# A fused attention, MoE and Fourier-mixing kernel: attention's steps, their router and the hand-over to the experts in another order

## The chip, the cores and the metric

The kernel runs on one core of one Trainium2 chip, in one launch. The metric is the device time of that launch in microseconds, as the median of the runs. The engines are TensorE (PE, with its weight loads PEld), VectorE (DVE), ScalarE (ACT), GpSimd (POOL) and SyncE (SP); SP issues most transfers, and a queue's waits are shown as SPq or POOLq.

## What is computed

Three layers follow each other: decayed attention without a softmax, a mixture of eight experts in which a token takes one expert, and a Fourier mixing with a channel MLP.

```python
# 1: q, k, v are (4, 8, 576, 64)
scores = scale * np.matmul(q, k.transpose(0, 1, 3, 2))
Dmat = np.where(rel >= 0, gamma[:, None, None] ** rel[None, :, :], 0.0)
x = np.matmul(scores * Dmat[None, :, :, :], v)          # as (4, 576, 512)
# 2: per token; e is its own argmax, or its predecessor's if the local gate is at least 0.5
logits = np.einsum('bsd,de->bse', x, w_gate)
local_gate = 1.0 / (1.0 + np.exp(-np.einsum('bsd,de->bse', x, w_local).squeeze(-1)))
out[b, s] = p[e] * (np.maximum(x[b, s] @ w1[e], 0.0) @ w2[e])
# 3
u = x + np.real(np.fft.fft(np.fft.fft(x, axis=1), axis=2))
out = u + np.maximum(norm(u) @ w_ch1, 0.0) @ w_ch2
```

## The kernel before

**Attention's steps.** Each of the four batches is cut into blocks of 128 tokens; STEPS lists 18 steps, four for block 0 of each batch (c = 0), then four for each later block, and at last two steps with two half blocks each. Blocks of one batch are tied by a state: `sp` = v'ks (L458), added on DVE to the running `sum` (L468, for c = 0 a copy, L466), which the next block's outputs read. The loop over the 18 steps writes all engines' work in the order in which they execute it. Step i does, on PE, the outputs o of step i-1 (L495 to L509: qg times the state, and am times v), then sp and the products a = kT'qT (L480) of step i, then `tr` (L524), which turns x of step i-1 by an identity with the gate's columns beside it. DVE turns a into am (L484, times the decay, in two halves), ACT copies o into xT (L516), which `tr` reads. `prep` (L429) makes qg and ks on POOL, two steps ahead.

**back.** From `tr` DVE sums the router's logits L (L527), ACT takes the largest magnitude (Abs, L536), DVE makes a scale mx from it (L537 to L546), ACT writes the scaled row's high half xh (L547) and DVE the low half xl (L549) into the row xr.

**route.** Once per four steps `route` runs as a generator beside the steps: m, ls, t, fr, cc on DVE (L558 to L567), ex on ACT, `row` on PE (L578, cc transposed), sm (L582 to L585), kr, er, e (L591 to L598) on DVE, et, oh, then the ranks rk on PE (L616 to L634), the gate (L641), and c8, sl, slot (L643 to L648), carry (L650). The slots are the places to which POOL's `scatter` (L666) sends the rows by indirect DMA; `fetch` (L685) reads the first expert's rows (called expert 8 below) back transposed.

**Beside the steps.** The weights of expert 8 come in eight pieces of 512 KB. `hook` (L2278) issues a piece per step from step 2 on, and at step 0 four DMAs that fill the rows' buffer with zeros. `beside` (L2296) converts the pieces: ACT takes `absmax` (L239) and writes a float16 high part (`high`, L281), DVE the rest (`low`, L286). 15 products on zeros (`warm`, L717) run on PE ahead of step 0.

**The end.** After step 17 PE runs hidden(f) (L815), expert 8's first products; relu's low half is a DVE instruction (L833) per f. DVE casts the tally of the router to n_i (L2108), from which SP takes the order of the other experts. Then `outputs` (L836) runs 24 products for each of two row tiles: for each f wh by the high and low hidden rows, and wl by the high ones. SP meanwhile loads the next expert's weights (`w1.load`, L229), the padding (L1006) and the rows xt and mt of the next two experts (`fetch`, L1047 and L1060). All of SP's queue goes in the order written.

## Time and profile before

| | before |
|---|---|
| median of three runs | 790.78 us (790.6, 790.78, 798.08) |
| the profiled execution | 787.88 us |
| its span | 785.7 us |
| PE busy | 724.8 us, 92% of the span |
| DVE busy | 592.3 us, 75% |
| ACT busy | 411.8 us, 52% |
| POOL busy | 126.8 us, 16% |

The page's chain that ended last is "issue" for 25% of the span. Attention takes the first 110 us, expert 8 the stretch to about 136, and the other experts follow from 139.86 us on. Times in rows are microseconds from the span's start; a row is one instruction or a run of equal ones, and brackets give the engine's idle time ahead of it and what ended it.

### The profile page before, as it was taken

What the parts mean: (1) busy time and instruction counts of PE and PEld (TensorE: products, weight loads), DVE (VectorE), ACT (ScalarE), POOL (GpSimd) and SP (SyncE); (2) the same over time, 40 slices, a digit from 0 to 9 for tenths busy, and PEclk for the clock granted to TensorE, in tenths of its full rate; (3) what the DMA queues carried; (4) which work ended last, traced back from release to release, by engine and by line L of the source; (5) the groups of instructions that cost most, each with busy time, mean ns of one, the idle gap of its engine ahead of it and who ended that gap; (6) DMA issues with size and microseconds to landing.
All of it is one profiled execution on the core that took longest, in us unless ns stands there. A gap on an engine that the chain in (4) does not pass through costs nothing. (4 is left out here: it accounts for less than half of the span.)

```text
span 785.7 us, 17150 instructions
## 1 busy us (share of the span) xinstructions
PE 724.8 (92%) x6529; PEld 542.8 (69%) x6529; DVE 592.3 (75%) x1432; ACT 411.8 (52%) x829; POOL 126.8 (16%) x225
## 2 busy tenths in 40 slices
PE   8888898899999998879998999899899999999996
PEld 5677685655566555557644448778788888888885
DVE  3678888589889988857898969958876695646462
ACT  1356657378888797845847526426332451414140
POOL 3566443002102201113000011010010001010101
PEclk9999999899999999999999999999999999999998
DMA  9998449999998998964427276600550017110000
GB/s 296 355 305 293 154 115 309 295 315 344 293 360 304 270 352 287 262 235 149 136 77 240 102 214 232 175 28 2 170 150 2 28 62 195 28 55 2 28 2 27
DMA packets 91929, 142.27 MB, mean 181 GB/s; under 512 B 48116, under 2 KB 49017, under 8 KB 90814
## 3 DMA queue, kind: packets, MB, share of 16 engines
q1 hardware_dynamic: 87246, 126.78, 51.4%
q0 software_dynamic: 4592, 14.31, 5.0%
q8 instruction: 53, 0.87, 0.4%
q14 instruction: 38, 0.31, 0.1%
HBM read 97.55 MB, written 35.12 MB: 169 GB/s over the span
## 5 line engine op out<-in xcount | busy, mean ns | idle before, releaser
L1666 PE MATMUL g<-gxt,wh 128*128 128x256 f16 (+1 forms) x992 | 143.6, 284 | 2.6 <-DMA gxt<-un 1.4
L2011 PEld LDWEIGHTS <-hd 128*128 128x128 f16 x1176 | 114.2, 98 | 26.9 <-issue 7.1
L1666 PEld LDWEIGHTS <-wh 128*128 128x128 f16 x1056 | 102.8, 98 | 28.5 <-issue 4.9
L286 DVE SCALAR_TENSOR_TENSOR wl<-wst,ws,wh 128x1024 f16<-128x1024 f32 (+1 forms) x82 | 100.3, 1253 | 8.1 <-ACT wh L281 8.0
L281 ACT ACTIVATE wh<-wst,ws 128x1024 f16<-128x1024 f32 x80 | 89.0, 1140 | 26.1 <-DVE ws L274 25.7
L815 PE MATMUL ps<-xt,wh 128*128 128x320 f16 (+4 forms) x544 | 79.1, 284 | 8.1 <-DMA xt<-xs 5.8
L845 PE MATMUL ps<-wh,hid 128*128 128x512 f16 (+2 forms) x528 | 84.6, 302 | 0.2 <-ACT hid L831 0.2
L2011 PE MATMUL g<-wh,hd 128*128 128x256 f16 x448 | 78.3, 273 | 4.3 <-DVE u L2040 2.0
L1666 PE MATMUL g<-gxt,wl 128*128 128x256 f16 (+1 forms) x496 | 80.5, 285 | 0.0
L815 PEld LDWEIGHTS <-wh 128*128 128x128 f16 x640 | 57.5, 100 | 33.2 <-issue 13.8
L1872 POOL DMA_INDIRECT out<-u,orow x18 | 17.9, 993 | 383.9 <-DVE u L2040 284.8
L845 PEld LDWEIGHTS <-hid 128*128 128x128 f16 (+2 forms) x792 | 46.4, 100 | 42.4 <-issue 2.7
L239 ACT ACTIVATE wh<-wst 128x1024 bf16<-128x1024 f32 x66 | 69.3, 1050 | 7.7 <-DVE wst L311 5.2
L2040 DVE SCALAR_TENSOR_TENSOR u<-g,ffs,u 128x256 f32<-128x256 f32 (+1 forms) x63 | 34.1, 568 | 49.3 <-PE g L2011 48.7
L1982 DVE SCALAR_TENSOR_TENSOR s<-g,r 128x256 f32<-128x256 f32 x168 | 53.3, 374 | 23.4 <-ACT hd L1976 22.7
L1955 ACT ACTIVATE hd<-s 128x640 f16<-128x640 f32 x56 | 41.3, 737 | 47.8 <-DVE s L1982 47.8
L1975 ACT ACTIVATE r<-g 128x256 f32<-128x256 f32 x56 | 21.1, 378 | 84.0 <-PE g L1666 78.0
L2011 PE MATMUL g<-e,hd 128*128 128x256 f16 x504 | 59.9, 273 | 5.0 <-DVE u L2040 4.0
L859 POOL DMA_INDIRECT x<-y,mt x25 | 31.5, 1261 | 194.7 <-ACT y L857 149.7
L2011 PE MATMUL g<-wl,hd 128*128 128x256 f16 x224 | 61.1, 273 | 0.0
L1666 PEld LDWEIGHTS <-wl 128*128 128x128 f16 x528 | 51.9, 98 | 11.7 <-issue 1.1
L845 PE MATMUL ps<-wl,hid 128*128 128x512 f16 (+2 forms) x264 | 56.4, 302 | 0.0
(299 smaller groups left out, 1280.7 us busy)
## 6 DMA issues: line engine op xcount, KB each, us to landing
wst<-in_moe_w SPq DMA_DIRECT2D x64, 512.0 KB
raw<-in_ch SPq DMA_DIRECT2D x14, 1024.0 KB
qk<-in_qkv SPq DMA_DIRECT2D x18, 512.0 KB
vk<-in_qkv SPq DMA_DIRECT2D x16, 512.0 KB
pair<-ch SPq DMA_DIRECT2D x32, 256.0 KB
ch<-d SPq DMA_DIRECT2D x14, 512.0 KB
wst<-ch SPq DMA_DIRECT2D x14, 512.0 KB
u<-u SPq DMA_DIRECT2D x9, 512.0 KB
```

The source lines that it names most:

```text
L239: self.nc.scalar.activation(out=x, in_=t, func=ACTF.Abs, accum_out=self.am[:, j : j + 1])
L281: self.nc.scalar.activation(out=self.dst[0][:, j, :], in_=self.pieces[j], func=ACTF.Copy, scale=self.by(j))
L286: self.nc.vector.scalar_tensor_tensor(out=l[:, j, c], in0=self.pieces[j][:, c], scalar=self.by(j), in1=h[:, j, c], op0=ALU.mult, op1=ALU.s ...
L815: nc.tensor.matmul(out=ps, lhsT=m[:, k, 128 * f : 128 * f + 128], rhs=xt[:, x + k, :], start=(k == 0 and i == 0), stop=(k == 3 and i == last),
L845: nc.tensor.matmul(out=ps[r * j : r * j + r, 0:d], lhsT=hid[x][:, f, 128 * t : 128 * t + r], rhs=m[:, 4 + f // 2, c : c + d], start=(f == ...
L859: nc.gpsimd.indirect_dma_start(out=x2[:, :].rearrange("t (k d) -> (t k) d", k=k), out_offset=bass.IndirectOffsetOnAxis(ap=mt, axis=0), in_ ...
L1666: nc.tensor.matmul(out=ps, lhsT=m[:, k + 4 * (f // 8), 128 * (f % 8) : 128 * (f % 8) + 128], rhs=xt[x][:, k, :], start=(k == 0 and i == 0) ...
L1955: nc.scalar.activation(out=hd[:, 0, 2:7], in_=s, func=ACTF.Copy, scale=C2 / 2)
L1975: nc.scalar.activation(out=r, in_=p[:, 1:3], func=ACTF.Relu)
L1982: V.scalar_tensor_tensor(out=d, in0=x, scalar=0.0, in1=y, op0=ALU.max, op1=op)
L2011: nc.tensor.matmul(out=ps, lhsT=hid[k][:, y, x, :], rhs=E[w][m][k], start=(k == 0 and m == y == 0), stop=(k == 7 and y == 1),)
L2040: V.scalar_tensor_tensor(out=y, in0=p, scalar=fs[:, c : c + 1], in1=y, op0=ALU.mult, op1=ALU.add)
```

## The change

In words: (1) Nine warm-up products instead of 15; the constants' loads change places (kd ahead of v, the identity's copies made by ACT, both gates in one array, the rest after step 1), and the zero-fill and the weights' pieces come at later steps. (2) In a step a stands ahead of sp, am ahead of the sum; the state's copies go to ACT and behind xh; the logits stand behind Abs; `high` gets in ahead of xh and `low` ahead of L. (3) A router's first part is taken up in the step after, behind `scores`; its parts from kr and from c8 on come behind xl. (4) Two `low` parts that ran as four halves in steps 16 and 17 run whole after the tally. (5) Expert 8's second products take wl's last. (6) SP fetches expert 0's rows ahead of the eighth piece of weights.

```diff
-WARM = 15
-FILLED = 4
+WARM = 9
+FILLED = 5
...
-HALVES = {16: [(4, 0)], 17: [(5, 0)]}, {16: [(4, 1)], 17: [(5, 1)]}
...
-    load(0)
-    kd = const("kd", [128, 4, 8], src=A["kd"].rearrange("p (c h) -> p c h", c=4))
+    kd = const("kd", [128, 4, 8])
+    load(0, lambda: nc.sync.dma_start(out=kd, in_=A["kd"].rearrange("p (c h) -> p c h", c=4)))
     dec = const("dec", [128, H, 128], src=A["dec"].rearrange("p (h q) -> p h q", h=H))
+    idw, idn = const("idw", [128, 4, 137]), keep.tile([128, 128], FP32, name="idn")
+    nc.sync.dma_start(out=idn, in_=A["idn"])
+    nc.sync.dma_start(out=idw[:, :, 128:137], in_=A["gates"].rearrange("p (c e) -> p c e", c=4))
+    nc.scalar.copy(out=idw[:, :, 0:128], in_=idn.unsqueeze(1).to_broadcast([128, 4, 128]))
     load(1)
...
-    idw = const("idw", [128, 4, 137])
-    nc.sync.dma_start(out=idw[:, :, 0:128], in_=A["idn"].unsqueeze(1).to_broadcast([128, 4, 128]))
-    nc.sync.dma_start(out=idw[:, :, 128:136], in_=A["w_gate"].rearrange("(c p) e -> p c e", p=128))
-    nc.sync.dma_start(out=idw[:, :, 136:137], in_=A["w_local"].rearrange("(c p) e -> p c e", p=128))
-    idn = keep.tile([128, 128], FP32, name="idn")
-    nc.sync.dma_start(out=idn, in_=A["idn"])
     load(2)
...
-            if c == 0:
-                V.tensor_copy(out=total[b][0], in_=sp)
-            else:
+            if c > 0:
                 V.tensor_tensor(out=total[b][c % 2], in0=sp, in1=total[b][(c - 1) % 2], op=ALU.add)
-            if c == 3:
-                for g in range(2):
+
+            def keep_state():
+
+                if c == 0:
+                    nc.scalar.copy(out=total[b][0], in_=sp)
+                for g in range(2) if c == 3 else ():
                     r = slice(64 * g, 64 * g + 64)
                     nc.scalar.copy(out=apart[b][r, :, r], in_=total[b][1][r])
...
         nc.scalar.activation(out=xh.bitcast(BF16), in_=tr, func=ACTF.Abs, accum_out=mx[:, 0:1])
+        if i < N - 1:
+            logits()
...
         V.reciprocal(out=mx[:, 2:3], in_=pi)
+        yield
         nc.scalar.activation(out=xh, in_=tr, func=ACTF.Copy, scale=mx[:, 2:3])
...
             rate()
+        if c < 3:
+            yield "amid"
         kr = W("kr", [C, 128], BF16)
...
         V.tensor_tensor(out=gate[:, at], in0=ps, in1=sm, op=ALU.mult)
+        if c < 3:
+            yield "amid"
         c8 = W("c8", [128, 2, 8])
...
-        scores(i)
+        kept = scores(i)
+        for g in fresh:
+            next(g)
+        live.extend(fresh)
+        fresh.clear()
...
+        next(r, None)
+        kept()
...
         if i % 4 == 0 and i > 0:
-            live.append(route(i // 4 - 1))
-            next(live[-1])
+            if i < 16:
+                fresh.append(route(i // 4 - 1))
+            else:
+                live.append(route(i // 4 - 1))
+                next(live[-1])
...
-    first.low(6)
-    first.low(7)
+    for j in range(4, 8):
+        first.low(j)
...
+    parts = ((h, 0), (h, 1), (l, 0))
+    each = [(f, i) for f in range(8) for i in range(3)]
+    if lows:
+        each.sort(key=lambda p: (p[1] == 2, p))
...
-    for p in range(6, 8):
-        w1.load(p)
+    w1.load(6)
     fetch(0)
+    w1.load(7)
     fetch(1)
...
-                if i == 0:
+                if i == 3:
...
-                if 2 <= i < 10:
-                    w.load(i - 2)
+                if 4 <= i < 12:
+                    w.load(i - 4)
```

How the order changes at three places. On DVE, around step 5 of attention, where the first router's part stands. Names: m to cc are the router's first part, sum the state, am the decayed scores, L the logits and mx the scale of the turned row. Before:

```order
L558 TENSOR_REDUCE m<-L 128x4
L560 TENSOR_TENSOR ls<-L,m 128x32
L563 SCALAR_TENSOR_TENSOR t<-ls,c_rt 128x32
L565 TENSOR_REDUCE fr<-t 128x4
L567 SCALAR_TENSOR_TENSOR cc<-L,fr 128x4
L569 CAST cc<-fr 1x4
L468 TENSOR_TENSOR sum_1_182<-sp,sum_0_181 128x256
L484 TENSOR_TENSOR am<-a,c_dec 128x4x128 x2
L527 TENSOR_REDUCE L<-tr 128x9
```

With the change, at the same place:

```order
L466 TENSOR_TENSOR am<-a,c_dec 128x4x128 x2
L481 TENSOR_TENSOR sum_1_178<-sp,sum_0_177 128x256
L576 TENSOR_REDUCE m<-L 128x4
L578 TENSOR_TENSOR ls<-L,m 128x32
L581 SCALAR_TENSOR_TENSOR t<-ls,c_rt 128x32
L583 TENSOR_REDUCE fr<-t 128x4
L585 SCALAR_TENSOR_TENSOR cc<-L,fr 128x4
L587 CAST cc<-fr 1x4
L539 TENSOR_REDUCE L<-tr 128x9
```

The router's six instructions stand behind the step's am and sum instead of ahead of them; on PE `row`, which reads cc, stands where it stood, behind `tr` and ahead of the next outputs.

On DVE behind the tally of the router, ahead of expert 8's second products (wl_78 the low hidden rows, one instruction an f; wl_76 the low part of a piece of the weights). Before:

```order
L2107 TENSOR_REDUCE wh_77<-wh_77 1x21
L2108 CAST n_i<-wh_77 1x20
L833 SCALAR_TENSOR_TENSOR wl_78<-r,wl_78 128x256
L286 SCALAR_TENSOR_TENSOR wl_76<-wst,ws,wh_75 128x1024 x2
L833 SCALAR_TENSOR_TENSOR wl_78<-r,wl_78 128x256 x3
```

With the change:

```order
L2149 TENSOR_REDUCE wh_77<-wh_77 1x21
L2150 CAST n_i<-wh_77 1x20
L871 SCALAR_TENSOR_TENSOR wl_78<-r,wl_78 128x256
L285 SCALAR_TENSOR_TENSOR wl_76<-wst,ws,wh_75 128x1024 x4
L871 SCALAR_TENSOR_TENSOR wl_78<-r,wl_78 128x256 x3
```

Four whole parts instead of two stand between the low hidden rows of f = 4 and those of f = 5 to 7.

On SP, from the reading of n_i on (wst a piece of the next weights, xs<-z the padding, xt and mt the rows of expert 0). Before:

```order
L2115 TENSOR_LOAD n_i
L2115 ISA x2
L1006 ISA
L1006 DMA xs<-z 32x9x528
L229 ISA
L229 DMA wst<-in_moe_w 128x2x512
L229 ISA
L229 DMA wst<-in_moe_w 128x2x512
L1047 DMA_TRANSPOSE xt<-xs 128x4x128 x2
L1060 DMA mt<-xs 128x2
```

With the change:

```order
L2157 TENSOR_LOAD n_i
L2157 ISA x2
L1048 ISA
L1048 DMA xs<-z 32x9x528
L228 ISA
L228 DMA wst<-in_moe_w 128x2x512
L1089 DMA_TRANSPOSE xt<-xs 128x4x128 x2
L1102 DMA mt<-xs 128x2
L228 ISA
L228 DMA wst<-in_moe_w 128x2x512
```

The transposes and mt stand ahead of the eighth piece instead of behind it; the six pieces ahead of n_i keep their place in SP's queue.

## Rows read from the trace of the kernel before

**Rows 1.** PE by line, 5.3 to 30.07: count, busy, mean ns, idle, releaser.

```profile
L458 PE MATMUL sp<-vk,ks 128*64 128x64 f32 x80 | 3.4, 228 | 3.1 <-POOL ks L441 3.0
L509 PE MATMUL o<-am,vk 128*64 128x128 f32 x64 | 5.7, 282 | 0.9 <-DVE am L484 0.9
L717 PE MATMUL warm<-z 128*128 128x512 f16 x8 | 2.2, 420 | 0.0
```

**Rows 2.** Windows: length, each engine's busy time (instructions), clock, DMA share, GB/s.

```profile
core 0: us, PE busy (x) PEld busy (x) DVE busy (x) ACT busy (x) POOL busy (x), PEclk, DMA share, GB/s
1.79:5.30 3.51, 3.51 (x9) 1.30 (x10) 0.00 (x0) 0.26 (x1) 1.94 (x5) 1.00 0.95 278
5.30:30.07 24.77, 20.54 (x264) 16.28 (x262) 12.06 (x30) 6.14 (x13) 7.25 (x7) 1.00 1.01 323
75.48:99.70 24.22, 19.81 (x306) 17.39 (x306) 21.22 (x67) 16.63 (x31) 13.20 (x24) 1.00 0.51 150
139.90:145.30 5.40, 5.40 (x52) 5.40 (x52) 0.82 (x3) 0.95 (x4) 0.00 (x0) 0.50 0.88 168
346.65:350.06 3.41, 3.41 (x9) 1.18 (x10) 3.24 (x11) 3.17 (x6) 0.00 (x0) 0.50 0.82 259
505.40:511.10 5.70, 2.82 (x25) 2.34 (x24) 5.56 (x16) 0.91 (x2) 0.00 (x0) 1.00 0.36 106
```

**Rows 3.** PE by line in 30.07:52.53, 52.53:75.48 and 75.48:99.7, one after another.

```profile
L524 PE MATMUL tr<-c_idw,xT 128*128 128x137 f32 x33 | 5.0, 291 | 2.8 <-ACT xT L516 1.6 <-DVE xr L549 1.2
...
L524 PE MATMUL tr<-c_idw,xT 128*128 128x137 f32 x33 | 5.0, 291 | 3.3 <-DVE xr L549 2.2 <-ACT xT L516 1.0
...
L524 PE MATMUL tr<-c_idw,xT 128*128 128x137 f32 x33 | 5.1, 291 | 4.4 <-ACT xT L516 2.9 <-DVE xr L549 1.5
...
L578 PE MATMUL row<-c_cb,cc 128*4 128x128 bf16 x1 | 0.2, 217 | 0.0
```

**Rows 4.** Timeline of PE: start, length, instruction, count, idle time before it.

```profile
110.06 0.61 PE L815 MATMUL ps<-wh,wh 128*128 128x256 f16 x4
...
124.94 0.60 PE L845 MATMUL ps<-wh,wl 128*128 128x512 f16 x2
...
139.86 0.37 PE L815 MATMUL ps<-xt,wh 128*128 128x128 f16 x2 [4.05 <-DMA xt<-xs]
...
346.65 0.59 PE L845 MATMUL bank<-wh,hidl 128*128 128x512 f16 x1 [3.95 <-PEq L2169]
```

**Rows 5.** Timeline of ACT in step 14.

```profile
90.44 0.69 ACT L547 ACTIVATE xr<-tr,mx 128x512 f16<-128x512 f32 x1 [1.47 <-DVE oh L605]
91.03 1.14 ACT L281 ACTIVATE wh<-wst,ws 128x1024 f16<-128x1024 f32 x1
```

**Rows 6.** Timeline of DVE in steps 13, 14 and 16.

```profile
83.42 0.59 DVE L583 TENSOR_SCALAR sm<-sm 128x4 f32<-128x4 f32 x1
...
86.42 0.41 DVE L468 TENSOR_TENSOR sum<-sp,sum 128x256 f32<-128x256 f32 x1
86.75 1.28 DVE L484 TENSOR_TENSOR am<-a,c_dec 128x512 f32<-128x512 f32 x2
...
103.29 0.18 DVE L558 TENSOR_REDUCE m<-L 128x4 f32<-128x32 f32 x1
...
104.25 0.16 DVE L567 SCALAR_TENSOR_TENSOR cc<-L,fr 128x4 bf16<-128x4 f32 x1
```

**Rows 7.** Timelines of DVE and of SP's queue: the rows of experts 8 and 0.

```profile
97.48 0.17 DVE L648 CAST c_slot_i<-c_slot_f 128x4 int32<-128x4 f32 x1
...
106.37 2.69 SPq L685 DMA_TRANSPOSE wh<-xs  x2
...
131.29 3.15 SPq L1047 DMA_TRANSPOSE xt<-xs  x2
```

**Rows 8.** Timeline of DVE: a half part of low in step 16, then the end.

```profile
100.54 0.75 DVE L286 SCALAR_TENSOR_TENSOR wl<-wst,ws,wh 128x512 f16<-128x512 f32 x1
...
125.30 2.46 DVE L286 SCALAR_TENSOR_TENSOR wl<-wst,ws,wh 128x1024 f16<-128x1024 f32 x2
127.69 0.41 DVE L833 SCALAR_TENSOR_TENSOR wl<-r,wl 128x256 f16<-128x256 f32 x1
```

More of the change, by code (lines that the diff above doesn't have):

```diff
@@ L443, in prep @@
             )
+        if c > 0:
+            qg = wk.tile([128, 4, 128], FP32, tag="qg", name="qg", bufs=3)
+            for j in range(len(lanes)):
+                w = slice(n * j, n * j + n)
+                nc.gpsimd.tensor_tensor(out=qg[:, :, w], in0=qT[:, :, w], in1=qds[c][:, :, 0:n], op=ALU.mult)
         pre[i] = (qg, ks)
@@ L719, in attention, with turn @@
     prep(1)
-    live = []
-    def turn():
-        for g in list(live):
-            if next(g, "end") == "end":
+    live, fresh, amid = [], [], []
+    def turn(of=None):
+        for g in list(live if of is None else of):
+            said = next(g, "end")
+            if said == "end":
                 live.remove(g)
-    level(1)
+            if said == "amid":
+                amid.append(g)
     for i in range(N):
@@ L747, in attention @@
             load(i + 3)
-        if i % 4 == 1 and 2 <= i // 4 + 2 <= 4:
-            level(i // 4 + 2)
+        if i % 4 == 0 and i < 16:
+            level(i // 4 + 1)
+        if i == 1:
+            rest()
         turn()
         next(r, None)
+        turn(amid)
+        amid.clear()
         if i > FILLED:
@@ L1129, in moe @@
     for t in range(2):
-        out(weights(0), hid0, mt0, fs, t, n, (parts,) if t else (), partial(w1.spread, 0) if t else None, 0)
+        out(weights(0), hid0, mt0, fs, t, n, (parts,) if t else (), partial(w1.spread, 0) if t else None, 0, True)
     v = weights(2)
@@ L2312, in beside @@
                     w.low(i - 12)
-                for j in HALVES[0].get(i, ()):
-                    w.low(*j)
                 yield
@@ L2319, in beside @@
                     w.high(j)
-                for j in HALVES[1].get(i, ()):
-                    w.low(*j)
                 yield
```

88 lines of the change are left out of this document (48 added, 40 removed).

## The prediction

> **What bounds the kernel now.** I read the table of busy time first: TensorE (PE) is by far the busiest engine, and the chain that ended last is mostly issue time on PE, so what can be won is PE's waiting. I then listed PE's idle time line by line for the stretch that the change rewrites, attention and the hand-over to the experts (0 to 145 us), and looked in the timelines of VectorE (DVE), ScalarE (ACT) and SyncE (SP) at who ended each wait. Behind 145 us no edit touches anything and PE is nearly dense, so I carry a shift at expert 0 unchanged to the end.
>
> [...] In steps 0 to 4 PE waits 3.1 us at sp, nearly all for ks on GpSimd (POOL), whose v block comes late, and 0.9 us at o for am [rows 1], while the DMA engines are full (share 1.01) and DVE is busy only 12.06 of 24.77 us [rows 2]. In steps 5 to 16 `tr` waits 2.8, 3.3 and 4.4 us in three cycles of four steps, half of it for the copy xT on ACT and half for xl on DVE, and `row` waits nothing [rows 3]. [...]
>
> **Term 1, the start (steps 0 to 4).** Fewer loads and broadcasts of constants stand between qk1 and qk2, kd comes ahead of v, the zero-fill's four DMAs go from step 0 to step 3, the pieces of the first weights start two steps later, POOL makes ks ahead of qg, and a stands ahead of sp on PE. All of it aims at the 4.0 us of waits for ks and am. The bytes ahead of step 4 fall little and the engines are full, so it can't all vanish; and the state's first copy, which leaves DVE, now stands on ACT behind xh and ahead of xT, on the chain tr, Abs, L, mx, xh, xT. I take half, 2.0 us, with 0.5 and 3.0 as bounds. What the moves delay: a piece now has two steps instead of four until `absmax` reads it on ACT. At about 5 us a step that is some 10 us, and I cost it at nothing; if a piece is late, ACT waits for the difference, and behind it xT and `tr`.
>
> **Term 2, cycles of four steps.** The conversion `high` (1.14 us) now runs between Abs and xh, in the 1.47 us that ACT idles ahead of xh [rows 5], instead of between xh and xT: that takes about 1.1 us off xT in steps 11 to 14. The sum stands behind am, and kr, er, e and the slots behind xl, so `tr` waits less for DVE. Against it, the first part of the router, m to cc, moves from the end of step 4k to behind am and the sum of step 4k+1, while its reader `row` keeps its place on PE, between `tr` and the next outputs. From a's end DVE needs 1.3 us for am, 0.33 for the sum and 1.1 for m to cc, 2.7 in all [rows 6]. PE meanwhile has sp (3.4 us in five steps, 0.7) and tr (5.0 in four, 1.2) [rows 1, 3], and reaches `row` after 1.9. So `row` waits 0.8 us where it waited nothing; where small operations stretch as one did to 0.59 [rows 6], more, and I put the upper bound at 2.0. I take 1.5 a cycle, nearer to it, since POOL works on ks and qg in just these steps. In each of the first two cycles I leave some 0.4 of waits for xT, so they win 2.8 - 1.5 - 0.4 = 0.9 and 3.3 - 1.5 - 0.4 = 1.4. In the third DVE is busy 21.22 of 24.22 us [rows 2], and no DVE work leaves it: at most 3.0 can be won, and with the router's part in its busiest step I take 0.5. Sum 2.8 us, bounds 0 (the new waits eat all) and 5.5 (`row` at 0.8, little left over).
>
> **Term 3, the rows for hidden(0).** The first expert's rows hang on the slots of step 15: cast at 97.48, transposes issued at 106.37 [rows 7], first product at 110.06 [rows 4], 12.6 us that nothing shortens. The cast now stands behind xl (0.67 us), so it gains 0.7 less than the steps do: 2.0 + 2.8 - 0.7 is 4.1, and I say 4.0 us at hidden(0).
>
> **Term 4, expert 8's second products.** Four half parts of `low` go from steps 16 and 17 (0.75 us each) to behind the tally's cast, as two whole parts ahead of the low hidden rows f5 to f7. Two parts took 2.46 us, so f5's rows, which started at 127.69, start 2.46 later and are there at about 130.5 [rows 8]. The block has 48 products from 124.94 to 135.81 (the wait ahead of 139.86 taken off), 0.226 each [rows 4]; with the wl products last PE wants f5's low rows after eleven, at 127.4. It waits 3.1 us and ends the block near 138.7 instead of 135.8. The DVE time freed earlier lies where hidden(0) waits for rows, so I count nothing for it. [...]
>
> **Term 5, rows for expert 0.** The two transposes leave their place behind the eighth piece. SP issued them at 131.29 [rows 7], and xt was read at 139.86 [rows 4], 8.6 us later. Now pieces 4 and 5 wait for `low` 4 and 5, the seventh for `low` 6 (125.30 + 3 x 1.23 = 129.0 [rows 8]), then come the transposes: issue about 129.5, landed by 138.1 at the same latency, sooner without 512 KB ahead of them. PE comes at 138.7, so the 4.05 us wait is gone, and the low clock behind it. But 3.1 us of idle time now lie inside expert 8's products. After 3.95 us idle [rows 4] the clock stood at 0.50 for 3.41 us; a stretch with 2.9 us idle in two pieces kept 1.00 [rows 2]. I count one such stretch, 1.7 us, with 0 and 2.7 as bounds.
>
> **The sum**, at expert 0: before, 139.86 and 2.7 lost behind it, 142.6. After, 138.7 - 4.0 + 1.7 = 136.4. Gain 6.2 us. The profiled execution took 787.88 us, its span 785.7; the sum takes it to about 781.7. The median of the runs, 790.78, lies 2.9 above that execution; less 6.2 it is **784.6 us**. With all terms at their low ends the gain is 0.5 + 0 - 0.7 + 3.9 - 2.7 = 1.0, at their high ends 3.0 + 5.5 - 0.7 + 3.9 = 11.7.
>
> **Rivals.**
> *Attention gives all, and the clock holds.* Term 1 at 2.3, term 2 at 4.5, no half-rate stretch: 2.3 + 4.5 - 0.7 + 3.9 = 10.0, 780.8. For it: the xT waits can go by order alone. Against: DVE is busy 88% in the third cycle.
> *The waits only change their name.* `row` waits 2.0 us a cycle, DVE is the bound in all of them, and term 1's 0.7 is taken back by the slots: nothing at hidden(0). The wait in expert 8 brings the longer clock loss: 3.9 - 2.7 = 1.2, 789.6. For it: the 10.5 us were split evenly over two engines, and relief of one leaves the other.
> *Slower: the clock at the start.* Nine warm-up products instead of 15. Until 5.30 us nine of them took 3.51 us [rows 2], 0.39 each where expert 8's take 0.226, so they ran near the lower level (though the clock column says 1.00 there). If the clock does not hold behind so short a lead, steps 0 to 4 run at half speed for a while: their PE work is 20.54 us [rows 2] less the warm-up's 2.2 [rows 1], 18.3 or 3.7 a step, and each such step costs 3.7 more, less the idle time in it. Term 1 is gone then; the other 4.2 us of gain are gone once the extra work passes the 4.0 us of idle time by 4.2, from 2.2 steps on. With all five steps it is 18.3 - 4.0 - 4.2 = 10.1 over before, 801. Against: the clock had risen by 5.30, with eight or nine of the 15 done, and from there to 30.07 it stood at 1.00 with 4.2 us idle. [...]
> *The fetch stays last.* If the transposes land at 140.0 as before, less 4.0, PE at 136.4 waits for nothing either, or 1.3 us if the clock held: inside the forecast's spread.
>
> **How the numbers follow.** Forecast 0.47 (own range 781.5 to 788), all of attention 0.25 (777.5 to 782.5), renamed waits 0.21 (788 to 792), slow start 0.05, anything else 0.02. A change of 1% (7.9 us, about what a measurement of this kernel can tell from none) lies at 782.9 and 798.7. Below fall nearly all of the second case and a sixth of the first, 0.32; above only part of the slow start, 0.04. Range 778 to 791.
>
> **What would show it.** Step 4's outputs start on PE near 28 us; `row` waits 1 to 2 us three times, and `tr` no more than 1 us in each of cycles one and two; hidden(0) starts near 106; a wait of about 3 us for DVE's hidden rows lies between two products of expert 8, and none for xt ahead of expert 0. If `tr` still waits for xl, term 2 is wrong; if expert 0 waits for xt over 1 us, term 5; if the block of expert 8 is dense, term 4; if PE is busy for well over 20 us of the time to step 5, the slow start is there.

## The result, and the profile after

| | before | changed |
|---|---|---|
| median of 20 runs each | 791.92 us (788.0 to 798.08) | 795.82 us (790.96 to 801.7) |
| the profiled execution | 787.88 us | 800.71 us |
| its span | 785.7 us | 798.9 us |
| its mean granted clock | 0.988 | 0.979 |
| PE busy / DVE / ACT / POOL | 724.8 / 592.3 / 411.8 / 126.8 us | 733.1 / 591.6 / 413.7 / 129.5 us |
| step 4's outputs start | 30.1 us | 29.94 us |
| step 16's outputs start | 99.8 us | 102.81 us |
| hidden(0) starts | 110.06 us | 114.38 us |
| expert 8's second products, expert 0, expert 1 start | 124.94, 139.86, 152.95 us | 130.21, 146.06, 156.86 us |

The change takes 1.0052 times as long as before, with the interval from 1.0031 to 1.0074: about 4 us lost where 6.2 were to be won, and 4.8 us above the range. The profiled execution lies 4.9 us above the median of the changed kernel; its distance at expert 1, 3.9 us, is that of the medians, and what it loses behind expert 1 is its own in large part (see What stays open).

PE by line in the three cycles of four steps, one after another (columns as in [rows 3]), and sp in the start:

```profile
L473 PE MATMUL sp<-vk,ks 128*64 128x64 f32 x80 | 3.4, 227 | 3.2 <-POOL ks L439 2.3 <-issue 0.4 <-POOL qg L446 0.4
...
L532 PE MATMUL tr<-c_idw,xT 128*128 128x137 f32 x33 | 5.1, 292 | 0.0
...
L596 PE MATMUL row<-c_cb,cc 128*4 128x128 bf16 x1 | 0.2, 218 | 1.9 <-DVE cc L587 1.9
...
L532 PE MATMUL tr<-c_idw,xT 128*128 128x137 f32 x33 | 5.0, 290 | 1.5 <-DVE kr L611 1.5
...
L596 PE MATMUL row<-c_cb,cc 128*4 128x128 bf16 x1 | 0.2, 218 | 1.0 <-DVE cc L585 1.0
...
L532 PE MATMUL tr<-c_idw,xT 128*128 128x137 f32 x33 | 5.0, 288 | 5.1 <-ACT xT L524 3.4 <-DVE kr L611 1.8
...
L596 PE MATMUL row<-c_cb,cc 128*4 128x128 bf16 x1 | 0.2, 217 | 0.8 <-DVE cc L585 0.8
```

`row` waits 1.9, 1.0 and 0.8 us where it waited nothing. `tr` waits nothing in the first cycle and 1.5 in the second, where [rows 3] had 2.8 and 3.3, but 5.1 in the third, where it had 4.4. The 3.1 us of [rows 1] at sp have become 3.2.

Windows of the changed kernel (columns as in [rows 2]): a stretch inside the start, one inside the third cycle, and one inside expert 8.

```profile
11.20:14.60 3.40, 3.40 (x30) 3.00 (x28) 0.00 (x0) 0.59 (x1) 0.61 (x1) 0.50 0.99 389
...
96.60:100.00 3.40, 3.40 (x33) 3.07 (x32) 2.97 (x13) 2.73 (x6) 0.18 (x1) 0.50 0.02 5
...
137.50:140.90 3.40, 3.40 (x10) 1.19 (x9) 0.98 (x7) 0.00 (x0) 0.00 (x0) 0.50 1.06 297
```

The start has a stretch at a granted clock of 0.50 that [rows 2] don't have, the third cycle another, 1.5 us behind the end of a wait of 2.56 us (at 95.08, shown below). Timeline of PE at the hand-over, answering [rows 4]:

```profile
114.38 1.04 PE L853 MATMUL ps<-wh,wh 128*128 128x256 f16 x4 [1.62 <-DMA wh<-xs]
...
135.80 1.77 PE L887 MATMUL ps<-wh,wl 128*128 128x512 f16 x5 [3.06 <-DVE wl L871]
...
146.06 1.11 PE L853 MATMUL ps<-xt,wh 128*128 128x128 f16 x17
```

The wait inside expert 8 is there with 3.06 us, half rate behind it (the window at 137.50), and expert 0 starts without the 4.05 us.

All of PE's time can be sorted into idle time (gaps in its timeline), what half rate cost (an estimate: half of the busy time at a granted clock of 0.50; the first 52 products of expert 0 take 5.46 us at it before, 3.14 in g3 of the experiments) and work (the rest), in us, from 1.79 on. Up to 5.30 us before and 7.81 in the changed kernel the clock column says 1.00, but products take longer than later (16 of a at 5.75 take 2.20 us in the changed kernel, 1.16 later), so I count PE's busy time there as half rate, 1.76 and 3.01 us of the first row:

| stretch | before: idle / half rate / work | changed: idle / half rate / work | difference |
|---|---|---|---|
| to step 4's outputs | 4.23 / 1.76 / 22.28 | 3.53 / 4.72 / 19.90 | -0.1 |
| to step 16's outputs | 10.54 / 0 / 59.15 | 10.57 / 1.71 / 60.59 | +3.2 |
| to hidden(0) | 0.36 / 0 / 9.94 | 1.62 / 0 / 9.94 | +1.3 |
| to expert 1 | 6.09 / 2.70 / 34.11 | 5.09 / 3.04 / 34.35 | -0.4 |
| to the end | 37.9 / 3.4 / 591.4 | 43.2 / 7.1 / 591.8 | +9.2 |

In the twelve steps from step 4 to 16 the idle time is what it was, 10.5 us under other names. Two columns of this table had no term in the prediction's attention: half rate (+4.7 up to step 16) and work (+1.4 in the twelve steps). The table sets one execution beside one, and its first row does not hold for others (see Point by point); in the twelve steps the difference does: they take 68.1 to 70.0 us in three traces that have before's steps up to there (before, and e3 and g3 of the experiments) and 72.9 to 73.5 in three that have the changed ones (changed, e4, g4).

### The profile page after: what moved, and what is told of

Its sections match the earlier page's. It is cut to its first block, busy times and chain, and to the rows that moved or that the text cites. A ratio compares the mean times of both kernels' runs of the same rounds, so it can differ in the third digit from the quotient of the medians.

```text
span 798.9 us, 17114 instructions
## 1 busy us (share of the span) xinstructions
PE 733.1 (92%) x6523; PEld 545.8 (68%) x6523; DVE 591.6 (74%) x1426; ACT 413.7 (52%) x834; POOL 129.5 (16%) x225
## 5 line engine op out<-in xcount | busy, mean ns | idle before, releaser
L285 DVE SCALAR_TENSOR_TENSOR wl<-wst,ws,wh 128x1024 f16<-128x1024 f32 x80 | 100.1, 1283 | 7.5 <-ACT wh L280 6.2
L280 ACT ACTIVATE wh<-wst,ws 128x1024 f16<-128x1024 f32 x80 | 89.1, 1141 | 31.7 <-DVE ws L273 31.6
L1914 POOL DMA_INDIRECT out<-u,orow x18 | 17.9, 996 | 384.0 <-DVE u L2082 286.2
L2082 DVE SCALAR_TENSOR_TENSOR u<-g,ffs,u 128x256 f32<-128x256 f32 (+1 forms) x63 | 34.1, 567 | 49.3 <-PE g L2053 47.5
L2053 PE MATMUL g<-e,hd 128*128 128x256 f16 x504 | 61.6, 277 | 5.0 <-DVE u L2082 4.0
```

The source lines that it names most:

```text
L280: self.nc.scalar.activation(out=self.dst[0][:, j, :], in_=self.pieces[j], func=ACTF.Copy, scale=self.by(j))
L285: self.nc.vector.scalar_tensor_tensor(out=l[:, j, c], in0=self.pieces[j][:, c], scalar=self.by(j), in1=h[:, j, c], op0=ALU.mult, op1=ALU.s ...
L1914: nc.gpsimd.indirect_dma_start(out=out[:, :], out_offset=bass.IndirectOffsetOnAxis(ap=orow[:, r // 128 : r // 128 + 1], axis=0), in_=o, in ...
L2053: nc.tensor.matmul(out=ps, lhsT=hid[k][:, y, x, :], rhs=E[w][m][k], start=(k == 0 and m == y == 0), stop=(k == 7 and y == 1),)
L2082: V.scalar_tensor_tensor(out=y, in0=p, scalar=fs[:, c : c + 1], in1=y, op0=ALU.mult, op1=ALU.add)
```

## The experiments

The second column is the ratio to the kernel before, run on the same chip. The third is the mean time of a run at half rate, worked out from each run's mean granted clock and span, (1 - clock) x 2 x span, an estimate that takes the clock to be either 1.00 or 0.50, the levels of the windows above; before has 22.6 to 23.7 us, the changed kernel 29.7. It counts the time at that level whether PE works or stands idle.

| label | ratio, 95% interval | us at half rate |
|---|---|---|
| e1_start | 1.0005 [0.9970, 1.0040] | 27.4 |
| e2_steps | 1.0081 [1.0046, 1.0115] | 33.3 |
| e3_end | 0.9999 [0.9976, 1.0023] | 19.5 |
| e4_warm15 | 1.0047 [1.0027, 1.0067] | 24.7 |
| f1_sm_late | 1.0036 [1.0007, 1.0066] | 31.7 |
| f2_route_old | 1.0021 [0.9997, 1.0045] | 32.3 |
| f3_qg_first | 1.0089 [1.0063, 1.0114] | 32.1 |
| f4_xh_only | 0.9986 [0.9955, 1.0017] | 22.1 |
| g1_sp_first | 1.0147 [1.0096, 1.0198] | 30.4 |
| g2_mended | 1.0130 [1.0082, 1.0178] | 34.1 |
| g3_fill | 1.0002 [0.9975, 1.0029] | 17.9 |
| g4_all_fill | 1.0103 [1.0052, 1.0154] | 34.8 |
| h1_scores | 1.0007 [0.9985, 1.0030] | 22.6 |
| h2_router | 1.0019 [0.9998, 1.0041] | 23.3 |
| h3_amid | 1.0094 [1.0059, 1.0128] | 32.9 |
| h4_start_xh | 0.9976 [0.9953, 0.9998] | 20.7 |
| i1_no_amid | 1.0067 [1.0039, 1.0095] | 32.5 |
| i2_no_amid15 | 1.0026 [0.9997, 1.0055] | 25.3 |

### The change in three pieces, and its warm-up

e1 is the kernel before with the start alone (part 1 of the change), e2 with the steps and the router (2 and 3), e3 with the end (4 to 6); e4 is the changed kernel with 15 warm-up products.

```diff
 e4, to the changed kernel
-WARM = 9
+WARM = 15
```

> Only part 1 of the change (nine warm-up products, constants' loads reordered, zero-fill and weight pieces later), all else as before. Theory 'the lead is too short' (in the changed kernel's trace the clock rose at 7.8 instead of 5.3 us and the first a products took 2.20 us instead of 1.16): 1 to 3 us over before, o of step 0 no earlier than 10.2. Theory 'the steps are at fault': within 1 us of before or 1 to 2 faster, step 4's outputs at 28 to 29 instead of 30.07.

> Only part 2 and 3 (order inside the steps, router in the step after, slots behind xl, ks ahead of qg on POOL), all else as before. Theory 'the steps are at fault' (router operations on DVE stand beside POOL's ks and qg and stretch; the third cycle, steps 13 to 16, grew from 24.3 to 27.7 us): 3 to 5 us over before, hidden(0) 2 to 4 later than 110.06, a wait of 1 to 2 us at row three times. Theory 'the lead is too short': 0 to 3 us faster than before.

> Only parts 4 to 6 (low parts after the tally, wl's products last, rows ahead of the eighth piece), all else as before. Forecast's own terms 4 and 5: a wait of about 3 us for DVE's hidden rows inside expert 8, none for xt, expert 0's first products at full clock: 2 to 3 us faster. Rival 'the wait only moves': a half-rate stretch of 3.41 us behind the new wait, 0 to 1 us faster than before or none.

> The changed kernel with 15 warm-up products again. Theory 'the lead is too short': clock at 1.00 from 5.3 us on, first a products 1.2 us long, 2 to 3 us faster than the changed kernel (793). Theory 'the steps are at fault': within 1 us of the changed kernel (795 to 796), since the six products more only fill PE's wait for ks.

The steps lose 0.81% by themselves; start and end give nothing that these runs can tell. So the rewritten steps are enough for the loss, and the nine warm-up products are not its cause: with 15 the whole change is as slow (1.0047). Part 2 as e2 has it includes an edit that the list of the change does not name: POOL makes ks ahead of qg. e2's longest wait stands around step 9, DVE, then POOL, then PE:

```profile
55.91 2.53 DVE L575 TENSOR_TENSOR ls<-L,m 128x32 f32<-128x32 f32 x1
...
55.08 0.99 POOL L685 DMA_INDIRECT xs<-xr,c_slot_i  x1 [0.28 <-POOL xr L683]
...
56.14 1.03 POOL L436 TENSOR_TENSOR ks<-vk,c_kd 128x512 f32<-128x512 f32 x1
57.14 1.25 POOL L443 TENSOR_TENSOR qg<-qk,qd 128x512 f32<-128x512 f32 x1
...
59.16 0.22 PE L593 MATMUL row<-c_cb,cc 128*4 128x128 bf16 x1 [3.27 <-DVE cc L582]
```

ls works on 32 elements a partition and takes 0.19 us where POOL is not in its way. Here it begins while POOL sends off a scatter, and ends at 58.44, when ks and qg are both through (58.39): 2.3 us of standing still, and `row`, which I had at 1.5 a cycle, waits 3.27. DVE did not get in between ks and qg here. By the rows ls began 0.23 us ahead of ks; what held it over that time they don't show.

This wait is not the loss by itself. The twelve steps of e2 have 10.3 us of idle time, where before has 10.5; what they have more is 3.4 us of half rate (a granted clock of 0.50 from 59.3 to 62.7, right behind this wait, where 16 products of o take 1.97 us instead of 1.09, and from 90.0 to 93.4) and 1.5 of work.

### Which operation is held

The changed kernel has the same with another instruction. DVE, POOL and PE around step 13:

```profile
83.98 2.70 DVE L603 TENSOR_TENSOR sm<-sm,c_pinv 128x4 f32<-128x4 f32 x1
...
83.34 0.99 POOL L688 DMA_INDIRECT xs<-xr,c_slot_i  x1 [0.28 <-DMA qk<-in_qkv]
...
84.40 1.03 POOL L439 TENSOR_TENSOR ks<-vk,c_kd 128x512 f32<-128x512 f32 x1
85.40 2.62 POOL L446 TENSOR_TENSOR qg<-qk,qd 128x512 f32<-128x512 f32 x3
...
87.49 1.18 PE L532 MATMUL tr<-c_idw,xT 128*128 128x137 f32 x8 [1.76 <-DVE kr L611]
```

The kernel before, at the same place:

```profile
84.25 0.75 DVE L585 TENSOR_TENSOR sm<-sm,c_pinv 128x4 f32<-128x4 f32 x1
...
82.43 1.55 POOL L437 TENSOR_TENSOR qg<-qk,qd 128x512 f32<-128x512 f32 x1
83.94 1.04 POOL L441 TENSOR_TENSOR ks<-vk,c_kd 128x512 f32<-128x512 f32 x1
```

There POOL was ahead: the sm of [rows 6], 0.59 us, ends when qg does, the next, 0.75, when ks does, so DVE got in between the two. Now sm begins 0.35 us before a scatter's issue ends and 0.42 ahead of ks, and it takes the whole pair on itself; xl stands behind sm, and `tr` behind xl.

Such a hold is not new. The kernel before has one in its second cycle, around step 9, DVE and PE, where POOL's qg and ks run from 59.65 to 61.90:

```profile
60.16 1.77 DVE L583 TENSOR_SCALAR sm<-sm 128x4 f32<-128x4 f32 x1
...
63.95 1.18 PE L524 MATMUL tr<-c_idw,xT 128*128 128x137 f32 x8 [1.76 <-DVE xr L549]
```

`tr` waits 1.76 us behind it, as long as in the changed kernel. So a held sm is no mark of the slow versions: h4 below, the fastest of all, has the same (1.79, and 1.77 at `tr`). Nor is the length of a hold fixed. In the 20 traces, between 30 and 110 us, some 60 small DVE instructions are held by the first of POOL's ks and qg, one right behind the other; some 25 of them are held until the second ends, the others only until the first does. What decides between the two I did not find.

The step behind it shows how the rest of the third cycle's waits come about, DVE, ACT and PE of the changed kernel:

```profile
90.62 1.76 DVE L285 SCALAR_TENSOR_TENSOR wl<-wst,ws,wh 128x1024 f16<-128x1024 f32 x1
...
93.03 0.69 ACT L565 ACTIVATE xr<-tr,mx 128x512 f16<-128x512 f32 x1 [2.47 <-DVE oh L625]
93.62 0.80 ACT L489 COPY sb<-sum 64x256 f32<-64x256 f32 x2
...
95.08 1.21 PE L532 MATMUL tr<-c_idw,xT 128*128 128x137 f32 x8 [2.56 <-ACT xT L524]
```

The change put `low` ahead of L, and here `low` itself is held (1.76 instead of 1.28, beside another qg on POOL from 89.89 to 91.31). L, mx and then xh are late: ACT stands 2.47 us ahead of xh, where it stood 1.47 in [rows 5], although `high` has been done by then. And behind xh come the state's copies, 0.80 us that stood ahead of Abs before, and only then xT. So in this step term 2's gain for xT, by `high` ahead of xh, was eaten by two other moves of the same change on the same chain.

Four edits of the changed kernel followed from this: f1 puts sm behind xl, f2 takes the router's first part back to the end of step 4k, f3 turns POOL's pair round, and g1 takes sp ahead of a again; g2 is f1, f2 and g1 together. f4 is the kernel before with xh behind `high`, and nothing else.

```diff
 f1
-        if c < 4:
+        if c == 3:
...
-        else:
+        if c != 3:
 f2
-            if i < 16:
-                fresh.append(route(i // 4 - 1))
-            else:
-                live.append(route(i // 4 - 1))
-                next(live[-1])
+            live.append(route(i // 4 - 1))
+            next(live[-1])
 f3, taken from behind ks to ahead of it
+        if c > 0:
+            qg = wk.tile([128, 4, 128], FP32, tag="qg", name="qg", bufs=3)
...
 g1, taken from behind the products of a to ahead of them
+        b, c = lanes[0]
+        if c < 4:
+            sp = p1.tile([128, 4, 64], FP32, tag="st", name="sp")
...
 f4
+        yield
         nc.scalar.activation(out=xh, in_=tr, func=ACTF.Copy, scale=mx[:, 2:3])
```

> The changed kernel, but sm's four small DVE instructions stand behind e (and so behind xl) in the routers of the first three cycles. Theory 'POOL holds DVE' (in the changed kernel single sm instructions of 0.17 us last 2.40 and 2.70 us, just as long as POOL's ks and qg run, and xl and tr wait behind them, 1.54 and 1.76 us): those two waits at tr vanish, 2 to 3.5 us faster than the changed kernel, 792 to 794. Rival 'DVE is simply full in the third cycle': no change, 795 to 796, since the same work is done.

> The changed kernel, but the router's first part (m to cc) back at the end of step 4k, all else changed. Theory 'row is the cost': the waits of 1.9, 1.0 and 0.75 us at row vanish, 3 to 4 us faster than the changed kernel, 792. Theory 'POOL holds DVE': sm still stands ahead of xl and is held as before, 0 to 2 us faster, 794 to 796.

> The changed kernel, but POOL makes qg ahead of ks again. Theory 'POOL holds DVE': the pair takes as long (2.3 us) and starts when qk and v are there, so the hold is the same or moves by 0.3 us, within 1.5 us of the changed kernel. Rival 'ks first costs, since it waits for v and qg behind it': 2 us or more faster than the changed kernel, and qg's place shows in the wait at o.

> The kernel before with one edit: xh behind the high part (one more yield in back), so that xT follows xh at once. Forecast's reading of term 2: xT 1.1 us earlier in steps 11 to 14, the 2.9 us of waits for xT in the third cycle shrink to about 1, 1 to 2 us faster than before. Rival 'DVE is simply full in the third cycle': tr then waits for xl instead, no change.

> The changed kernel, but PE does sp ahead of a again (DVE keeps am ahead of the sum). In the traces PE's working time, its waits taken off, is 19.6 and 19.7 us for four steps with sp first and 20.1 and 20.4 with a first. Theory 'a first costs PE time': that difference goes (0.1 to 0.2 us a step, some 2 us over 16 steps), 1 to 3 us faster than the changed kernel, 793 to 795. Rival 'only waits and the clock count': working time back to 19.7, but am later by sp's 0.6 us and the waits longer by as much, no change, 795 to 796.

> The changed kernel with the three parts undone that the runs so far point at: the router's first part back in step 4k, sm behind xl, sp ahead of a. Start, xh's order and the end stay changed. If their costs add (about 2.5, 1.3 and 2 us), 789 to 791, level with before or 1 to 2 us faster. If the loss lies in the half-rate stretches, which none of the three removes by itself, 793 to 795.

f1 holds sm for 0.75 us at most, and its steps 8 to 16 take 47.5 us instead of 50.9; but the first cycle, where cc and a cast now take 0.99 and 1.19 and `row` waits 2.96, goes from 22.0 to 25.9, and the ratio falls only from 1.0052 to 1.0036, within both intervals. This is the nearest to a test of the holds, and it speaks against them as the whole cause: with the long ones gone, f1's twelve steps wait 8.1 us instead of 10.6, but they lose 4.8 us to half rate instead of 1.7. f2 gives back the most, and its interval reaches below 1; yet in it ls is held for 2.12 us and sm for 1.97. f3 is the worst of the three. So each edit moved the meetings, none removed them. f4 can't be told from before.

g1 and g2 failed as experiments on this: from step 1's outputs to step 4's a step takes 5.46 us, where the changed kernel's takes 4.37. In g1 PE waits 1.22 us at sp (at 32.89), and the profile names nothing that ended the wait. By the code, and not by a run, sp has one buffer, which the state's copy empties; the change put that copy on ACT behind xh, which a later sp bears and an earlier one doesn't. These two edits belong together, and my expectation that their prices add up was wrong.

### The three edits of the steps alone

h1 is the kernel before with part 2's order of a step (a ahead of sp, am ahead of the sum, the copies on ACT, ks ahead of qg, the logits behind Abs), h2 with the router's first part moved, h3 with the parts from kr and from c8 on behind xl; h4 is before with the new start, 15 warm-up products, and f4's edit.

```diff
 h2, to the kernel before
-            live.append(route(i // 4 - 1))
-            next(live[-1])
+            if i < 16:
+                fresh.append(route(i // 4 - 1))
...
 h3, to the kernel before
+        if c < 3:
+            yield "amid"
         kr = W("kr", [C, 128], BF16)
...
+        if c < 3:
+            yield "amid"
         c8 = W("c8", [128, 2, 8])
...
+        turn(amid)
+        amid.clear()
```

> The kernel before with the products' part alone: a ahead of sp, am ahead of the sum, the state's copies on ACT, ks ahead of qg, logits behind Abs; xh and router as before. Theory 'a first costs PE time, the copies' chain costs little': PE's working time 0.5 us more in each group of four steps, 1 to 3 us slower. Theory 'the router's place is the loss': within 1 us of before, or 1 us faster by the start's waits for ks.

> The kernel before with the router's first part behind the next step's products alone. Theory 'the router's place is the loss': waits of 1 to 3 us at row in three steps instead of none, tr's waits smaller by half of that, a half-rate stretch behind the longest, 3 to 5 us slower. Rival: row's waits only replace tr's, within 1 us of before.

> The kernel before with kr, er, e and the slots behind xl alone. Forecast: tr's waits for xl shrink by 0.5 to 0.8 us in three steps each, but the slots of step 15 are later by 0.7: within 1 us of before, or 1 us faster. Theory 'the parts only lose together': no change here.

> The kernel before with the start's new order (15 warm-up products kept) and xh behind the high part. If term 1's gain is real and only the short lead took it back: 2 to 3 us faster, 788 to 789. If PE's early waits just move to later steps: within 1 us of before.

h3 alone loses 0.94%, as much as the whole change or more (the intervals overlap). POOL, DVE and PE of h3 around step 13:

```profile
77.74 1.04 POOL L670 DMA_INDIRECT xs<-xr,c_slot_i  x1 [1.91 <-DVE sum L468]
...
78.83 1.24 POOL L667 COPY xr<-c_pos 128x1 int32<-128x1 int32 x1
...
81.53 1.25 POOL L437 TENSOR_TENSOR qg<-qk,qd 128x512 f32<-128x512 f32 x1
82.75 1.03 POOL L441 TENSOR_TENSOR ks<-vk,c_kd 128x512 f32<-128x512 f32 x1
...
82.17 1.66 DVE L560 TENSOR_TENSOR ls<-L,m 128x32 f32<-128x32 f32 x1
...
84.62 1.21 PE L524 MATMUL tr<-c_idw,xT 128*128 128x137 f32 x8 [3.19 <-ACT xT L516]
```

And of the kernel before, where the scatter went at 75.77:

```profile
76.83 1.35 POOL L437 TENSOR_TENSOR qg<-qk,qd 128x512 f32<-128x512 f32 x1
78.14 1.04 POOL L441 TENSOR_TENSOR ks<-vk,c_kd 128x512 f32<-128x512 f32 x1
...
79.19 0.19 DVE L560 TENSOR_TENSOR ls<-L,m 128x32 f32<-128x32 f32 x1
...
80.17 1.21 PE L524 MATMUL tr<-c_idw,xT 128*128 128x137 f32 x8 [1.02 <-ACT xT L516]
```

The slots are ready later (their cast begins at 76.76, ahead of the sum that the profile names), so the scatter waits 1.91 us, and what stands behind it in POOL's order comes later too: a copy that takes 0.18 elsewhere takes 1.24 while DVE runs `low` (78.75 to 80.03), so that here POOL's is the one held, and qg and ks begin 4.7 and 4.6 us later, where ls, by the steps' lag alone, is 3.0 later. Before, ls came just behind the pair; here it falls into it; ACT's ex, which reads ls and stands ahead of xT, waits 1.57 us for it, and `tr` waits 3.19 instead of 1.02. I had priced the slots by what they do to SP's fetch (term 3, 0.7 us) and never looked at what stands behind the scatter on POOL.

h4 is faster than both kernels, 0.24%, the only version here whose interval lies below 1, and that just; its hidden(0) starts at 109.16.

### The slots' edit taken out of the whole change

i1 is the changed kernel without that edit, i2 the same with 15 warm-up products.

```diff
 i1 and i2
-        if c < 3:
-            yield "amid"
...
 i2
-WARM = 9
+WARM = 15
```

> The changed kernel with one piece undone: the router's parts from kr and from c8 on stand ahead of the step's own work again, not behind xl. Alone, that piece cost 0.94%. If it is the cause in the whole change too, tr waits under 1 us in cycle two, step 16's outputs come near 100 us instead of 102.8, and the median falls by 0.5 to 1% to the kernel before or just under it: ratio 0.995 to 1.000. If the loss is shared with the others (row's wait for the moved first part, the sums behind am), step 16 stays behind 102 us and the ratio at 1.003 to 1.006.

> The same with 15 warm-up products again. If the start's half-rate stretch is a cost of the nine, o(4) comes 1 to 2 us earlier than in the run beside it and the ratio falls by another 0.1 to 0.2%, to about 0.996, below both kernels. If the stretch comes and goes from run to run whatever the count, the two runs agree within their intervals.

My theory that this edit is the cause fell: without it the changed kernel is no faster (1.0067). DVE, POOL and PE of i1:

```profile
85.53 2.68 DVE L603 TENSOR_TENSOR sm<-sm,c_pinv 128x4 f32<-128x4 f32 x1
...
85.94 1.03 POOL L439 TENSOR_TENSOR ks<-vk,c_kd 128x512 f32<-128x512 f32 x1
86.94 2.62 POOL L446 TENSOR_TENSOR qg<-qk,qd 128x512 f32<-128x512 f32 x3
...
89.87 1.18 PE L532 MATMUL tr<-c_idw,xT 128*128 128x137 f32 x8 [2.60 <-DVE xr L567]
```

The same sm meets the same pair, and since kr, er and e now stand between it and xl, `tr` waits 2.60 instead of 1.76. The edit is enough for the loss when alone, and not needed for it in the whole change. i2 lies 0.4% lower than i1, but e4 had shown 0.05% for the same six products; their intervals overlap, and the warm-up's share stays open. The time at half rate is shorter with 15 in both pairs, 25.3 us against 32.5 and 24.7 against 29.7. And i2 has the longest hold of all, DVE at the same sm:

```profile
85.93 4.05 DVE L603 TENSOR_TENSOR sm<-sm,c_pinv 128x4 f32<-128x4 f32 x1
```

It ends at 89.98, when ks and three qg of POOL are through (89.96), and `tr` waits 3.96 us behind it, in a version that is among the less slow (1.0026).

### The end: does a gain at expert 0 reach the end?

g3 is the kernel before with 34 idle products in the wait ahead of expert 0; g4 the changed kernel with 26 such products ahead of f5's low rows in expert 8.

```diff
 g3, to the kernel before
+    full, wh = bank()[:, 0:256], weights(0).dst[0]
+    for _ in range(34):
+        nc.tensor.matmul(out=full, lhsT=wh[:, 0, 0:128], rhs=wh[:, 0, 0:256], start=True, stop=True)
 g4, to the changed kernel
+        if (f, i) == (5, 1) and callable(lows):
+            lows()
+        for _ in range(26):
```

> The kernel before with 34 products of 256 columns on PE, into a bank that nobody reads, ahead of expert 0: they fill 3.7 of the 4.05 us in which PE waits for xt. Theory 'the half-rate stretch at expert 0 costs 2.7 us': no half-rate stretch at 138 to 145, expert 0's first 48 products at 0.055 instead of 0.11 us, 2 to 3 us faster up to expert 1. Theory 'a gain in front of expert 1 is given back, since DVE there waits for the raw weights': those 2 to 3 us come back as a wait of PE for DVE's hidden rows in expert 1 (none before, 2.5 us in the end alone), and the median stays within 1 us.

> The changed kernel with 26 such products where PE waits 3.06 us for f5's low rows in expert 8. No half-rate stretch at 134 to 141 us, expert 0 up to 1.7 us earlier. Theory 'given back in expert 1': no gain in the median, 795 to 796. Theory 'the half-rate stretches are the loss': 1 to 2 us faster, 794.

g4 filled nothing: its products themselves waited 3.53 us, named after ACT's r, and then ran 3.00 us that the kernel has to pay, so it tells nothing of the clock. g3 did as meant. PE of g3 at expert 0:

```profile
137.32 3.88 PE L1134 MATMUL ps<-wh 128*128 128x256 f16 x34
141.92 1.95 PE L815 MATMUL ps<-xt,wh 128*128 128x128 f16 x32 [0.72 <-DMA xt<-xs]
```

Expert 0's products run at full clock (0.061 us each over 32, where before has 0.112 at a granted clock of 0.50), and it takes 10.8 us instead of 13.1. Yet the time is that of before, 1.0002. e3 tells the same with the changed end: from hidden(0) to expert 1 it needs 40.71 us instead of 42.89, and its ratio is 0.9999. Where the gain goes stands in expert 1, PE and DVE of e3:

```profile
161.33 0.86 PE L814 MATMUL ps<-xt,wh 128*128 128x416 f16 x4 [1.54 <-DVE hid L832]
168.80 0.86 PE L814 MATMUL ps<-xt,wh 128*128 128x416 f16 x4 [0.98 <-DVE hid L832]
...
150.45 0.69 DVE L298 TENSOR_SCALAR d<-raw 128x1024 int32<-128x1024 int32 x1 [2.85 <-DMA raw<-in_ch]
```

PE waits 1.54 + 0.98 us for the hidden rows there, and DVE, which makes them, has stood 2.85 us for the raw channel weights. Before, neither waits: DVE began that instruction at 149.59 without idle time. The transfer sets a pace that an earlier expert 0 does not change: 2.5 us of new waits stand against 2.2 won, 20 us behind them. From hidden(0) to the second products of expert 1 it is 60.0 us before, 60.5 in e3 and 59.8 in g3. In the changed kernel it is 62.5, with 3.0 us lost to half rate in expert 8 and waits of 1.56 + 0.98 in expert 1: there the new end does not give back what the steps lose, it adds to it. Nine traces with the changed steps and end (all but g4) have 61.0 to 62.5, nine with the end of before 59.5 to 61.6.

## Why the prediction was wrong

**What failed first: the waits of term 2.** The term left 1.9, 1.9 and 3.9 us of waits in the three cycles, 7.7 in all. Idle time stayed at 10.6, and that is 2.9 of the 6.0 us by which the term was out (2.8 to be won, 3.2 lost); the work and the half rate below are the rest. `row` came out near the forecast, 1.9, 1.0 and 0.8 for three times 1.5. What the term had wrong is why `tr` waits for xl. I read that wait as the order of DVE's work; in the second cycle of before 1.76 of its 3.3 us stand behind a held sm (60.16 above). The change leaves sm ahead of xl, so the hold stayed, with 2.40 us around step 9 (59.80) and 2.70 at 83.98, and `tr` still waits 1.5 in cycle two. In cycle three it waits 5.1: 1.76 behind the second of these, and 2.56 for an xT that `low` ahead of L and the state's copies made late.

The price of a hold was wrong too. I took up to 2.0 us a cycle from one small operation that stretched to 0.59 [rows 6]. That row was no bound: it was an sm that met qg's last half microsecond, and the same trace has the 1.77. In these traces one instruction lost up to all that POOL had in a row (ks and one qg in the changed kernel's 2.70, ks and three qg in i2's 4.05), and POOL's row was there to be read: qg and ks with 1.35 and 1.04 us (76.83 and 78.14 above). Shown: the holds, and the waits right behind them. Not shown: that they make the loss; against it stand the idle time of e2 and of the changed kernel, f1, and the hold of i2.

**Work that I counted at nothing.** Putting a ahead of sp costs PE itself. Outputs, sp and a of a step before, and outputs, a and sp with the change:

```profile
82.47 1.09 PE L509 MATMUL o<-am,vk 128*64 128x128 f32 x16
83.40 0.63 PE L458 MATMUL sp<-vk,ks 128*64 128x64 f32 x16
83.96 1.16 PE L480 MATMUL a<-qk 64*128 64x128 f32 x16
```

```profile
82.92 1.09 PE L517 MATMUL o<-am,vk 128*64 128x128 f32 x16
83.95 1.16 PE L462 MATMUL a<-qk 64*128 64x128 f32 x16
85.04 0.69 PE L473 MATMUL sp<-vk,ks 128*64 128x64 f32 x16
```

From the outputs' start to the last end it is 2.65 us before and 2.81 now. Over twelve steps that would be 1.9 us, the table has 1.4; h1, which has this order on the kernel before, shows work of 20.1, 20.4 and 20.3 us in the three cycles where before has 19.6, 19.7 and 19.9, and e1, without it, has those of before. The second cycle parts all 20 traces: 19.5 to 19.7 us of work with sp first, 20.3 to 20.5 with a first. As a whole h1 is not slower (1.0007): its twelve steps wait 9.2 us instead of 10.5, and step 4's outputs start early (below).

**The clock.** Term 5 counted one stretch at half rate, 1.7 us, and it came as counted. The others were not counted: one in the start, one behind that 2.56 us wait in cycle three, one at hidden(0) behind the fetch. Over all runs the changed kernel is at half rate 29.7 us instead of 23. Half of the difference, 3.4 us, is by the same estimate the most that this can have cost, since half rate costs nothing while PE stands idle; the medians lie 3.9 apart. Over the 127 runs of before that were made beside the experiments, a microsecond more at half rate goes with 0.39 us more of time; by that, an estimate from a correlation, the 6.7 us would be 2.6.

Where half rate comes from is shown in part. The waits of the twelve steps did not grow in sum, they were gathered into longer ones. In the traces of before, e1, e3, f4, g3 and h4 no wait there is longer than 1.77 us, and the clock stays at 1.00. In the changed kernel the stretch from 96.6 to 100.0 stands behind a wait of 2.56, in e2 one from 59.3 to 62.7 behind 3.27, in i2 one from 92.5 to 95.9 behind 3.96, and in f1 one of 6.8 us begins inside the wait of 2.96 that ends at 38.02. But 2.77 us in e4 and 2.93 in h2, both at `row`, and the 3.19 in h3 have none behind them. So a long wait can cost more than its length, and that is a way in which moving waits costs time; I have no run that holds the clock and leaves the waits. Nor does time at half rate rank the versions: f1 and f2, with 1.0036 and 1.0021, have as much of it as e2, h3 and i1 (32 to 33 us).

**Point by point.** Step 4's outputs start at 29.94, not near 28 (term 1), and the wait at sp is what it was. But 30.07, from which the 28 was counted, is the earliest of five traces with the start of before (before, e3, g3, h2, h3: 30.07 to 32.59, mean 31.6); five with the changed start (changed, f1, f2, g4, i1) have 29.09 to 30.11, mean 29.6. That is the 2.0 us of term 1, and luck: by the means the waits that the term was to shorten gave 0.6, work fell by 2.3, the six warm-up products among it, and half rate rose by 0.9. The gain goes with a ahead of sp and ks ahead of qg, which e2 and h1 have without the new start (28.80 and 29.11), rather than with the loads: e1 and h4, which have the new start without them, have 31.66 and 30.43. So e1 tests only a part of term 1, and its interval (0.9970 to 1.0040) does not exclude the 0.9975 that 2.0 us would be. Term 2 was to win 2.8 and lost 3.2, the difference of 6.0 being 2.9 of waits that stayed, 1.4 of work and 1.7 of half rate. Term 3's 0.7 became 1.3, with a fetch wait of 1.62. Hidden(0) starts at 114.4 instead of 106.1. Terms 4 and 5 held: 3.06 us of wait against 3.1, no wait for xt, one stretch of 3.40 us at 0.50; the end alone won 2.18 us from hidden(0) to expert 1 where terms 4 and 5 make 3.9 - 1.7 = 2.2. The 2.7 us that the sum counts as lost behind 139.86 are an estimate too, half of the 5.40 at a granted clock of 0.50 [rows 2]; no run shows them, and g3, whose expert 0 runs without that stretch, shows 2.3 (10.8 us for 13.1). In the whole change this gain is 0.4 (42.5 us for 42.9), since a second stretch at half rate, from hidden(0) on, came to it. And the step ahead of all terms, "I carry a shift at expert 0 unchanged to the end", failed: e3 and g3 give their gains back in expert 1, and the changed kernel loses 2.5 us more than it had lost at hidden(0). PE was nearly dense there because the transfers had come early enough, with little to spare: 2.2 us won brought 2.5 us of waits in e3, and 2.0 brought 1.6 in g3.

**The rivals.** In attention it was the second that came nearest, "the waits only change their name": 10.57 us of idle time for 10.54. Its 789.6 left out work and clock, and kept 1.2 us of the end's gain. Half rate in the start came, as in the third rival, for 3.4 us beyond the first 6.0 and not for whole steps; traces with the start of before have such a stretch as well (e3 from 27.9, h2 from 28.2); with 15 products the whole is no faster, so it was not the short lead that decided. I gave all of slower by over 1% a chance of 0.04, and the median did not go there; but my range ended 0.2 us above no change at all, though the two sums that carried it, terms 2 and 3, rested on one stretched row and on SP's queue alone.

**What stays open.** What brings each half-rate stretch, and so how the loss of 4 us parts into waits, work and clock. Whether undoing the router's move helps more in the whole (1.0021) than the move costs alone (1.0019): the intervals allow the same size. And a difference of single executions behind expert 1: at about 300 us PE waits for xt 1.77 us in the profiled run of before and 5.55 in that of the changed kernel, which is part of the 9.2 us of the table's last row. It is 5.57 in e3, 1.69 in f4, and 1.14 in e4, which has the whole change, so the change does not bring it each time; I did not find what makes it.

## What to carry over

Before moving a small instruction on VectorE, set its new place beside GpSimd's row of operations, not only beside the engine that waits for it, and price a meeting between a few tenths of a microsecond and the sum of all that GpSimd has back to back, since both occur here (0.59 us for an sm in [rows 6], 4.05 for one in i2); a row in which the meeting was short is no bound. Look first for the holds that the kernel has already: a wait that stands behind one (1.76 us at `tr`, before and with the change) did not go away by order alone. When a step is moved later, follow every queue behind its reader (here the scatter on POOL, and behind it the next ks and qg), since in h3, where the scatter waited 1.91 us, what is written after it came later too, qg by 4.7. Before a gain is carried to the end, find the next thing that arrives by transfer and how early it is. Count PE's work and its time at the lower clock beside its waits: here the sum of the waits did not move. And before a difference of two traces is believed, set beside it what several executions of the same code differ by, 2.5 us in this start.
